# Turning float64 weights into float32: the low word rounded on ScalarE, added to the bits on GpSimd

## The chip, the core and the metric

One core of a Trainium2 chip runs the whole program. The metric is device time of one execution, in microseconds (us); the time of a kernel is the median of its runs. The engines are TensorE (PE in the profile; PEld are its weight loads), VectorE (DVE), ScalarE (ACT), GpSimd (POOL) and the queue engine SyncE (SP), which issues most transfers.

## What is computed

Three layers follow each other. A retention layer (4 batches, 8 heads, 768 positions, head size 64) keeps a decaying state and gives 3072 tokens of 512 features. A first expert layer and a second, gated one follow:

```python
def _moe_ref(x, w_in, w_out):            # 512 -> 2048 -> 512
    h = x @ w_in
    g = h * (1.0 / (1.0 + np.exp(-1.702 * h)))
    return (g @ w_out).astype(np.float32)

def _moe2_ref(x, w_gate, w_val, w_out):  # 512 -> 1536 -> 512
    gate = 1.0 / (1.0 + np.exp(-(x @ w_gate)))
    val = x @ w_val
    return (gate * val @ w_out).astype(np.float32)
```

The weights arrive as float64. The kernel gets them as 64-bit words and makes float32 values of them on the chip.

## The kernel before, in words

**Stages.** The 24 steps of 128 positions of the retention layer are cut into pieces ("items": scores, state update, output). Four steps run first, as a lead-in (9 to 26.7 us). Then 96 units follow, each one tile of 128 hidden features of the first expert layer for one block of 512 tokens: `proj` (L270) multiplies the input by the unit's weights in 12 matmuls, `gated` (L277) applies the sigmoid, and `emit_out` (L359) multiplies by the output weights, two units later (`DEPTH = 2`). Units 0 to 7 (block 0, features 0 to 7; `WHOLE`) use whole float32 output weights in slower matmuls (L375). Other operands are split into a rounded part and a rest: `split_w` (L262) casts on ACT (`wh`, L265) and subtracts on POOL or DVE (`wl`, L266). Retention items for the next block lie between the units' steps: in units 0 to 5 (block 1), and again from unit 24 on. The second expert layer fills the span from about 641 us.

**Conversion.** `stage` (L202) loads a tile of 128 x 512 words of 64 bits into one of 4 buffers. `convert` (L210) returns its steps. `scale` (ACT, L228) multiplies the upper 32 bits, read as float32, by 2^-112, which sets the exponent right. `upper` (DVE) shifts the bits left by 3 (L233) and puts the sign bit back (L236). `lower` (DVE) masks the exponent of the result (L242) and multiplies the lower 32 bits by 2^-52 and by that power of two (L246). `total` (L256) adds the two in float32. There are 68 tiles: 32 of the first layer (18 of them by the end of unit 7, two per unit in units 0 to 7 and then one per unit in units 8 to 21), whose `total` runs on POOL, and 36 of the second layer (5 in 8 units, units 22 to 79), whose `total` runs on DVE and is written to memory (`w2d`). `cva` has 3 buffers, `cvb` 2.

**Order.** The program is scheduled by hand: each engine runs its instructions in the order of the code, and a tile's readers and writers wait for each other. The loop over units (L735) puts the steps of `conv` and `conv2` between the unit's other steps:

```python
            conv[0]()          # L758: ACT, first tile
            conv2[0]()         # ACT, second tile
            conv[1]()          # DVE
            if i < FH:         # FH = 8
                conv[2]()      # DVE
                conv[3]()      # POOL
```

After these come the unit's `proj`, the split of the next unit's weights, the sigmoid and the items, and `conv2`'s remaining steps close the unit. The score matmuls (L144) share three PSUM banks `h` with `proj`, and so wait for the gate product (DVE, L284) that empties one.

Of the kernel before, what the change touches and what calls it, by code (L numbers as in the profile page):

```python
# [8 lines left out]
F32 = mybir.dt.float32  # L9
F32R = mybir.dt.float32r  # L10
U32 = mybir.dt.uint32
U64 = mybir.dt.uint64
AF = mybir.ActivationFunctionType
ALU = mybir.AluOpType

P = 128
# [8 lines left out]
def retention_moe_moe2(  # L25
# [12 lines left out]
    nc = tc.nc  # L38
# [12 lines left out]
    def pool(stack, name, bufs, side, **kw):  # L51
        return stack.enter_context(tc.tile_pool(name=name, bufs=bufs, side=side, reuse_waits="tile", **kw))
# [9 lines left out]
    cv_p = pool(right, "cv", 2, "right")  # L62
# [35 lines left out]
    def load_next(s, *parts):  # L98
        for i in parts:
            if s < NSTEP and i not in in_t.get(s, {}):  # L100
                load_in(s, i, in_p, "in")
# [23 lines left out]
    def emit_decays(c):  # L125

        for a in range(KC):
            nc.scalar.mul(dq_sb[c - 1][:, a, :], dq_sb[max(c - 2, 0)][:, a, :], dg_sb[:, a:a + 1])
# [73 lines left out]
    def stage(n=1):  # L202

        for _ in range(min(n, len(to_stage))):
            ph, f, k = to_stage.popleft()
            t = cv_p.tile([P, 512], U64, name="w64", tag="w64", bufs=4)
            nc.sync.dma_start(out=t, in_=(w1 if ph == "1" else w2)[f, k])
            staged.append((ph, f, k, t))

    def convert(n, lo_engine):  # L210

        work = []
        for _ in range(min(n, len(staged))):
            ph, f, k, t = staged.popleft()  # L220
            words = t.bitcast(U32).rearrange("p (n two) -> p n two", two=2)
            a = cv_p.tile([P, 512], F32, name="cva", tag="cva", bufs=3)
            b = cv_p.tile([P, 512], F32, name="cvb", tag="cvb")
            work.append((ph, f, k, words[:, :, 0], words[:, :, 1], a, b))

        def scale():
            for ph, f, k, lo, hi, a, b in work:
                nc.scalar.mul(a, hi.bitcast(F32), 2.0 ** -112)  # L228

        def upper():  # L230
            for ph, f, k, lo, hi, a, b in work:
                ai = a.bitcast(U32)
                nc.vector.tensor_scalar(out=ai, in0=ai, scalar1=3, scalar2=None, op0=ALU.logical_shift_left)  # L233
            for ph, f, k, lo, hi, a, b in work:
                ai = a.bitcast(U32)
                nc.vector.scalar_tensor_tensor(  # L236
                    out=ai, in0=hi, scalar=0x80000000, in1=ai, op0=ALU.bitwise_and, op1=ALU.bitwise_or
                )

        def lower():  # L240
            for ph, f, k, lo, hi, a, b in work:
                nc.vector.tensor_scalar(  # L242
                    out=b.bitcast(U32), in0=a.bitcast(U32), scalar1=0xFF800000, scalar2=None, op0=ALU.bitwise_and
                )
            for ph, f, k, lo, hi, a, b in work:
                nc.vector.scalar_tensor_tensor(  # L246
                    out=b, in0=lo, scalar=2.0 ** -52, in1=b, op0=ALU.mult, op1=ALU.mult
                )

        def total():  # L250
            for ph, f, k, lo, hi, a, b in work:
                r = a
                if ph == "1":
                    r = wraw_p.tile([P, 512], F32, name="wraw", tag="wraw")
                    raw1[f, k] = r
                lo_engine.tensor_tensor(out=r, in0=a, in1=b, op=ALU.add)  # L256
                if ph == "2":
                    nc.sync.dma_start(out=w2d[f, k], in_=r)

        return scale, upper, lower, total  # L260

    def split_w(raw, lo_engine):  # L262
        wh = wsp_p.tile([P, 512], F32R, name="wh", tag="wh")
# [39 lines left out]
    def att_items(j):  # L303

        t0, n = blocks1[j]
        items = []
        for i in range(n // C):
            s = t0 // C + i

            def first(s=s, i=i):  # L310
                if i == 0:
                    alloc_x(j)
                emit_scores(s)
                if s >= 3:
                    load_next(s + 1, KN, V)

            def second(s=s):
                emit_update(s)
                if s >= 3:
                    load_next(s + 2, Q, K)  # L320

            def third(s=s, i=i):
                if s + 1 < NSTEP:
                    emit_prep(s + 1)
                emit_y(s, *x_t[j], i * C)

            items += [first, second, third]
        return deque(items)

    FH = F1 // 2
    segments = [(b, f0, f0 + FH) for f0 in (0, FH) for b in range(2)]
    segments += [(b, 0, F1) for b in range(2, len(blocks1))]
# [13 lines left out]
    def split_for(i):  # L348

        if i < len(units):  # L350
            b, f = units[i]
            w_t[i, 0] = split_w(raw1[f, 0], nc.gpsimd if i < 3 * FH else nc.vector)
# [33 lines left out]
    def evict1(b, f):  # L386
        acc = acc_t[b]
        for c in range(4):
# [8 lines left out]
            else:  # L397
                nc.vector.tensor_copy(t, acc[c])  # L398
            nc.sync.dma_start(out=(x2d if f == F1 - 1 else halfd)[b][:, c, :], in_=t)

    NG = NT // 1024  # L410
# [9 lines left out]
    def open_early():  # L420
        p2["x"] = pool(ctx, "x2", 1, "right")
        p2["xt"] = pool(ctx, "xt", 6, "right")
        p2["w"] = [pool(ctx, "we", 1, "right")]
# [74 lines left out]
    def load_chain(n):  # L498
        if n >= len(chains):
            return  # L500
        g, r, p, m = chains[n]
        f = 2 * (r * PAIRS + p)
        t = p2["w"][n % 2].tile([P, 8, 256], F32, name="raw8", tag="raw8")
        for ff, sl in ((f + 1, slice(A21, A22 + 1, 2)), (f, slice(A11, A12 + 1))):
            nc.sync.dma_start(out=t[:, sl, :], in_=w2d[ff, m].rearrange("p (a c) -> p a c", a=2))
        wraw8[n] = t
# [172 lines left out]
    with tc.manual_schedule():  # L679
# [31 lines left out]
        parts = deque()  # L711
        for n, it in enumerate(att_items(0)):
            if n in (3, 6):
                parts.extend(convert(1, nc.gpsimd))
                stage()
                parts.popleft()()
            it()
            if n == 2:
                load_next(4, KN, V)
            if n % 3 == 1:  # L720
                for _ in range(len(parts) - 1):
                    parts.popleft()()
                emit_decays(n // 3 + 2)
            if n % 3 == 2:
                while parts:
                    parts.popleft()()
            if n in (8, 10):
                split_for((n - 8) // 2)
# [6 lines left out]
        for i, (b, f) in enumerate(units):  # L735
            if i == 0:
                items = att_items(1)
            elif (b, f) == (1, FH):
                items = att_items(2)
            elif b > 1 and f == 0:  # L740
                items = att_items(b + 1) if b + 1 < len(blocks1) else deque()
                if b == len(blocks1) - 1:
                    assert not staged and not to_stage
                    right.close()
                    open_early()
                    xs = prep_x(0)
                    load_chain(0)
            first = staged and staged[0][0] == "1"
            conv, conv2 = ([lambda: None] * 4 for _ in range(2))
            if first:  # L750
                conv = convert(1, nc.gpsimd)
                if i < FH:
                    conv2 = convert(1, nc.gpsimd)
            elif staged and (5 * i) // 8 > (5 * (i - 1)) // 8:
                conv = convert(1, nc.vector)
            xh, xl = x_t[b]
            n = blocks1[b][1]
            conv[0]()  # L758
            conv2[0]()
            conv[1]()  # L760
            if i < FH:
                conv[2]()
                conv[3]()
            hb = psum_tile("h")
            proj(hb, w_t.pop((i, 0)), xh, xl, n)
            if i > 0:
                split_for(i + 1)
            split_out(i + 1)
            if i == len(units) - 1:
                split_out(i + 2)  # L770
            g_t[i] = gated(hb, n, i < WHOLE)
            if i >= FH:
                conv[2]()
            if items and (b < 2 or f >= 1):
                items.popleft()()
            gated_lo(g_t[i], n)
            if i >= FH:
                conv[3]()
            stage(4 - len(staged))
            if items and b < 2:  # L780
                items.popleft()()
            for step in conv2[1:]:
                step()
            pend.append(i)
            while pend and i - pend[0] >= DEPTH:
                emit_out(pend.popleft())
            next(xs, None)
            if b == len(blocks1) - 1:
                if f == 9:
                    sums(0)  # L790
                elif f in (11, 13):
                    split_chain(0, f == 13)()
# [144 lines left out]
```

## Time and profile before

| | |
|---|---|
| runs | 1194.47, 1196.26, 1196.8 us; median 1196.26 |
| profiled execution | 1195.28 us, its span 1193.5 |
| TensorE busy | 1175.5 us, 98% |
| VectorE | 790.7 us, 66% |
| ScalarE | 541.4 us, 45% |
| GpSimd | 534.6 us, 45% |
| transfers | 123.48 MB, 103 GB/s over the span |

Busy shares are means over stages. A busy TensorE can be one that runs slowly: its clock has two levels, 1.2 and 2.4 GHz, and the profile gives the granted clock as a share of the higher one. The first 200 us and the rest of the span have to be read apart.

### The profile page before, as it was taken

The numbers are of one execution on the slowest core, as the hardware profiler recorded it, in microseconds if no ns is written. First come the engines' busy times: TensorE is split into PE (matmuls) and PEld (weight loads), VectorE is DVE, ScalarE is ACT, GpSimd is POOL, SyncE is SP. The second block draws the span as 40 slices with busy tenths as digits, with TensorE's granted clock in tenths as the row PEclk, the third lists the DMA queues.
The fourth block names the chain that finished last, engine by engine and source line by source line (L and its number), as shares of the span: only waits on it lengthen the run. The fifth ranks groups of instructions, "written<-read, shape, count | busy, mean of one in ns | idle before, by whom it ended". The sixth has DMA issues, their size and how long they took to land.

```text
span 1193.5 us, 16042 instructions
## 1 busy us (share of the span) xinstructions
PE 1175.5 (98%) x5916; PEld 950.4 (80%) x5916; DVE 790.7 (66%) x1050; ACT 541.4 (45%) x948; POOL 534.6 (45%) x398
## 2 busy tenths in 40 slices
PE   7999999999999999999999999999999999999998
PEld 6656878888888888888788888888888888888887
DVE  6979999676687778766664535458535458535454
ACT  5424444444444444444554626264626164626161
POOL 5557875223232332332454625257635357635340
PEclk9989999999999999999999999999999999999999
DMA  9654245533425333412202212133212133212111
GB/s 327 208 163 141 89 159 160 189 129 125 141 88 166 124 126 115 139 65 80 71 1 76 85 36 71 36 109 117 92 36 71 36 102 120 90 42 62 46 36 71
DMA packets 62575, 123.48 MB, mean 103 GB/s; under 512 B 6816, under 2 KB 16288, under 8 KB 62496
## 3 DMA queue, kind: packets, MB, share of 16 engines
q1 hardware_dynamic: 61920, 121.54, 31.4%
q8 instruction: 46, 0.75, 0.3%
q10 hardware_dynamic: 576, 0.92, 0.2%
q14 instruction: 33, 0.27, 0.1%
HBM read 98.31 MB, written 24.12 MB: 103 GB/s over the span
## 4 chain that ended last, share of the span: by engine, by line
PE 91%; DVE 5%; issue 1%; POOL 1%; DMA 1%; ACT 1%; SPq 0%; DVEq 0%; ACTq 0%; POOLq 0%
PE pa L534 16%; PE pd L534 8%; PE acc L379 7%; PE h L275 7%; PE h L274 7%; PE h L273 7%; PE acc L381 6%; PE acc L380 6%; PE po L658 4%; PE po L657 4%; PE pb L534 4%; PE po L656 4%; PE h L144 2%; PE h L185 1%; DVE cva L236 1%; PE pd L657 1%
## 5 line engine op out<-in xcount | busy, mean ns | idle before, releaser
L266 POOL TENSOR_TENSOR wl<-wraw,wh 128x512 fp32r<-128x512 f32 x112 | 166.1, 1488 | 292.7 <-ACT wh L265 292.2
L273 PE MATMUL h<-xh,wh 128*128 128x512 f32 x384 | 153.7, 400 | 0.8 <-ACT xh L189 0.7
L275 PE MATMUL h<-xh,wl 128*128 128x512 f32 x384 | 151.2, 394 | 1.8 <-POOL wl L266 1.7
L274 PE MATMUL h<-xl,wh 128*128 128x512 f32 x384 | 150.2, 391 | 0.2 <-DVE xl L190 0.2
L379 PE MATMUL acc<-gh,wh 128*128 128x512 f32 x352 | 141.8, 403 | 1.4 <-DVE half L398 1.4
L381 PE MATMUL acc<-gl,wh 128*128 128x512 f32 x352 | 137.4, 390 | 0.0
L380 PE MATMUL acc<-gh,wl 128*128 128x512 f32 x352 | 137.3, 390 | 0.0
L265 ACT CAST wh<-wraw 128x512 fp32r<-128x512 f32 x184 | 109.2, 617 | 34.9 <-PE acc L381 33.7
L526 POOL TENSOR_TENSOR ol<-raw,oh 128x768 fp32r<-128x768 f32 x36 | 66.9, 1859 | 121.2 <-ACT oh L523 121.2
L284 DVE TENSOR_TENSOR sg<-h,sg 128x512 f32<-128x512 f32 x88 | 60.5, 688 | 87.6 <-ACT sg L283 87.5
L283 ACT ACTIVATE sg<-h 128x512 f32<-128x512 f32 x88 | 52.6, 597 | 143.3 <-PE h L275 143.2
L534 PE MATMUL pa<-xoh,oh 128*128 128x512 f32 x288 | 112.5, 391 | 0.0
L534 PE MATMUL pa<-xoh,ol 128*128 128x512 f32 x288 | 112.2, 389 | 0.0
L534 PE MATMUL pa<-xol,oh 128*128 128x512 f32 x288 | 112.1, 389 | 0.0
L289 ACT CAST gh<-sg 128x512 fp32r<-128x512 f32 x88 | 54.7, 621 | 98.3 <-DVE sg L284 98.3
L646 POOL TENSOR_TENSOR wol<-wor,woh 128x512 fp32r<-128x512 f32 x36 | 57.1, 1585 | 83.0 <-ACT woh L645 83.0
L275 PEld LDWEIGHTS h<-xh,wl 128*128 128x128 f32 x384 | 72.5, 189 | 20.4 <-POOL wl L266 4.9
L273 PEld LDWEIGHTS h<-xh,wh 128*128 128x128 f32 x384 | 72.5, 189 | 17.9 <-issue 1.0
L274 PEld LDWEIGHTS h<-xl,wh 128*128 128x128 f32 x384 | 72.4, 189 | 17.4 <-issue 1.9
L236 DVE SCALAR_TENSOR_TENSOR cva<-w,cva 128x512 uint32<-128x512 uint32 x68 | 82.7, 1216 | 2.3
L656 PE MATMUL po<-woh,g2h 128*128 128x512 f32 x216 | 84.0, 389 | 0.0
L657 PE MATMUL po<-wol,g2h 128*128 128x512 f32 x216 | 84.0, 389 | 0.0
(132 smaller groups left out, 2597.2 us busy)
## 6 DMA issues: line engine op xcount, KB each, us to landing
w<-in_w_dram SPq DMA_DIRECT2D x68, 512.0 KB, 3.7
in_t<-in_qkv_dram SPq DMA_DIRECT2D x93, 256.0 KB, 3.5
raw<-w2d SPq DMA_DIRECT2D x72, 256.0 KB, 3.2
w2d<-cva SPq DMA_DIRECT2D x36, 256.0 KB, 2.2
wor<-w2d SPq DMA_DIRECT2D x36, 256.0 KB, 2.7
out_dram<-ost SPq DMA_DIRECT2D x23, 256.0 KB, 2.0
xt<-x2d SPq DMA_DIRECT2D x18, 256.0 KB, 4.2
x2d<-ost SPq DMA_DIRECT2D x14, 256.0 KB, 2.9
```

The lines of the kernel that those rows point to most:

```text
L236: nc.vector.scalar_tensor_tensor(out=ai, in0=hi, scalar=0x80000000, in1=ai, op0=ALU.bitwise_and, op1=ALU.bitwise_or)
L265: nc.scalar.copy(wh, raw)
L266: lo_engine.tensor_tensor(out=wl, in0=raw, in1=wh, op=ALU.subtract)
L273: nc.tensor.matmul(bank[:, :n], wh[:, k, :], xh[:, k, :n], start=(k == 0), stop=False)
L274: nc.tensor.matmul(bank[:, :n], wh[:, k, :], xl[:, k, :n], start=False, stop=False)
L275: nc.tensor.matmul(bank[:, :n], wl[:, k, :], xh[:, k, :n], start=False, stop=(k == KC - 1))
L379: nc.tensor.matmul(a, wh[:, wc], gh[:, :n], start=st, stop=False)
L380: nc.tensor.matmul(a, wl[:, wc], gh[:, :n], start=False, stop=False)
L381: nc.tensor.matmul(a, wh[:, wc], gl[:, :n], start=False, stop=sp)
L534: nc.tensor.matmul(bank, w[:, kk], x[:, k, :], start=start and k == 0 and w is wh and x is xh, stop=stop and k == 1 and w is wl, skip_grou ...
L656: nc.tensor.matmul(bank, gh, wh, start=f == 0, stop=False)
L657: nc.tensor.matmul(bank, gh, wl, start=False, stop=False)
```

## The change

The lower word becomes a whole number of 0 to 8 on ACT (times 2^-29, written as a 32-bit integer), and GpSimd adds it to the float32 bits as integers; a carry out of the fraction runs into the exponent, as it should. DVE's mask and product are left out, and the second layer's `total` moves from DVE to GpSimd. `scale` now issues two ACT instructions per tile; `conv` has three steps, and `total` of units 0 to 7 stands where it stood.

```diff
-    def convert(n, lo_engine):
+    def convert(n):
@@
-            b = cv_p.tile([P, 512], F32, name="cvb", tag="cvb")
+            b = cv_p.tile([P, 512], U32, name="cvb", tag="cvb")
@@ scale
                 nc.scalar.mul(a, hi.bitcast(F32), 2.0 ** -112)
+            for ph, f, k, lo, hi, a, b in work:
+                nc.scalar.mul(b, lo, 2.0 ** -29)
@@
-        def lower():
-            for ph, f, k, lo, hi, a, b in work:
-                nc.vector.tensor_scalar(
-                    out=b.bitcast(U32), in0=a.bitcast(U32), scalar1=0xFF800000, scalar2=None, op0=ALU.bitwise_and
-                )
-            for ph, f, k, lo, hi, a, b in work:
-                nc.vector.scalar_tensor_tensor(
-                    out=b, in0=lo, scalar=2.0 ** -52, in1=b, op0=ALU.mult, op1=ALU.mult
-                )
@@ total
-                lo_engine.tensor_tensor(out=r, in0=a, in1=b, op=ALU.add)
+                nc.gpsimd.tensor_tensor(out=r.bitcast(U32), in0=a.bitcast(U32), in1=b, op=ALU.add)
@@ the loop over units
-            elif staged and (5 * i) // 8 > (5 * (i - 1)) // 8:
-                conv = convert(1, nc.vector)
+            elif staged and (5 * i) // 8 > (5 * (i - 1)) // 8:
+                conv = convert(1)
@@
             if i < FH:
                 conv[2]()
-                conv[3]()
@@
             g_t[i] = gated(hb, n, i < WHOLE)
-            if i >= FH:
-                conv[2]()
@@
             if i >= FH:
-                conv[3]()
+                conv[2]()
```

How the order moves. DVE, from the gate product of unit 1 to the end of that unit's second tile (`w_` and a number is a staged tile of words; names with a number differ between the two programs). Before:

```order
L284 TENSOR_TENSOR gw<-h,gw 128x512
L190 TENSOR_TENSOR xl<-h,xh 128x4x128
L148 TENSOR_TENSOR A<-h,dm_sb 128x512 x2
L233 TENSOR_SCALAR cva<-cva 128x512
L236 SCALAR_TENSOR_TENSOR cva<-w_325,cva 128x512
L242 TENSOR_SCALAR cvb<-cva 128x512
L246 SCALAR_TENSOR_TENSOR cvb<-w_325,cvb 128x512
```

The same place in the changed program (lines there are lower by some 3 to 22):

```order
L271 TENSOR_TENSOR gw<-h,gw 128x512
L190 TENSOR_TENSOR xl<-h,xh 128x4x128
L148 TENSOR_TENSOR A<-h,dm_sb 128x512 x2
L230 TENSOR_SCALAR cva<-cva 128x512
L233 SCALAR_TENSOR_TENSOR cva<-w_324,cva 128x512
```

Two of the tile's four DVE instructions are gone; the next gate product stands that much nearer.

ACT in unit 1, from the first tile's product to the sigmoid, with what each waits for. Before:

```order
L228 ACTIVATE cva<-w_267 128x512 [waits DMAHW5_49,DVE_49]
L228 ACTIVATE cva<-w_325 128x512 [waits DMAHW6_49,Pool_49]
L265 CAST wh<-wraw 128x512
L283 ACTIVATE gw<-h 128x512 [waits PE_49]
L189 CAST xh<-h 128x4x128 [waits PE_49]
```

And in the changed program:

```order
L223 ACTIVATE cva<-w_267 128x512 [waits DMAHW5_49,DVE_49]
L225 ACTIVATE cvb<-w_267 128x512 [waits Pool_49]
L223 ACTIVATE cva<-w_324 128x512 [waits DMAHW6_49,DVE_49]
L225 ACTIVATE cvb<-w_324 128x512 [waits Pool_49]
L252 CAST wh<-wraw 128x512
L270 ACTIVATE gw<-h 128x512 [waits PE_49]
L189 CAST xh<-h 128x4x128 [waits PE_49]
```

Each tile has one more ACT instruction, and it waits for POOL, for the `total` that last read its `cvb` buffer; the cast and the sigmoid are queued behind it.

## Rows read from the trace of the kernel before

**Rows 1.** the page: busy time of each engine, then the span in 40 slices

```profile
PE 1175.5 (98%) x5916; PEld 950.4 (80%) x5916; DVE 790.7 (66%) x1050; ACT 541.4 (45%) x948; POOL 534.6 (45%) x398
PE   7999999999999999999999999999999999999998
PEclk9989999999999999999999999999999999999999
```

**Rows 2.** table of stretches, one core; columns: stretch, length, PE, PEld, DVE, ACT, POOL busy (instructions), granted clock, DMA

```profile
9.00:26.70 17.70, 13.69 (x184) 11.23 (x184) 13.92 (x20) 13.04 (x35) 12.70 (x10) 1.00 1.03 389
26.70:94.00 67.30, 62.75 (x343) 41.66 (x344) 59.31 (x82) 23.89 (x43) 36.74 (x30) 0.92 0.53 179
36.80:45.10 8.30, 6.18 (x31) 4.63 (x30) 7.51 (x13) 2.35 (x4) 4.10 (x4) 0.79 0.56 190
62.60:72.60 10.00, 7.84 (x27) 4.36 (x25) 8.49 (x13) 2.33 (x4) 5.77 (x6) 0.66 0.47 158
102.00:146.50 44.50, 44.50 (x190) 35.44 (x189) 42.98 (x48) 22.16 (x40) 36.13 (x23) 1.00 0.35 116
146.50:182.60 36.10, 34.27 (x146) 26.68 (x145) 34.97 (x39) 18.01 (x34) 28.36 (x19) 1.00 0.46 145
182.60:260.00 77.40, 77.40 (x491) 63.25 (x491) 61.73 (x90) 34.40 (x63) 25.85 (x19) 1.00 0.50 162
1000.00:1100.00 100.00, 100.00 (x443) 82.46 (x442) 55.38 (x69) 48.02 (x79) 50.64 (x41) 1.00 0.23 71
```

**Rows 3.** list of waits, TensorE: what waited for what, us in total, times, longest

```profile
PE h L144 <- DVE gw L284: 4.1, 2, 2.2
PE acc L185 <- DVE A L148: 1.7, 4, 0.7
PE h L275 <- POOL wl L266: 1.7, 4, 1.2
PE acc L178 <- POOL qs L120: 1.7, 2, 1.0
PE acc L379 <- DVE half L398: 1.4, 1, 1.4
```

**Rows 4.** one line at a time: min/median/max duration in ns, first and last start, shapes

```profile
L233 DVE TENSOR_SCALAR cva<-cva x68: 416/421/1550, 13.9 to 551.3; 128x512 uint32<-128x512 uint32 x68
L236 DVE SCALAR_TENSOR_TENSOR cva<-w,cva x68: 691/1640/1822, 14.3 to 551.8; 128x512 uint32<-128x512 uint32 x68
L242 DVE TENSOR_SCALAR cvb<-cva x68: 408/426/1291, 15.0 to 555.4; 128x512 uint32<-128x512 uint32 x68
L246 DVE SCALAR_TENSOR_TENSOR cvb<-w,cvb x68: 691/693/1637, 15.5 to 555.8; 128x512 f32<-128x512 uint32 x68
L284 DVE TENSOR_TENSOR sg<-h,sg x88: 675/691/694, 100.0 to 642.8; 128x512 f32<-128x512 f32 x88
L296 DVE TENSOR_TENSOR gl<-sg,gh x88: 679/684/1522, 102.1 to 644.2; 128x512 fp32r<-128x512 f32 x88
L256 DVE TENSOR_TENSOR cva<-cva,cvb x36: 681/683/686, 189.4 to 557.0; 128x512 f32<-128x512 f32 x36
L256 POOL TENSOR_TENSOR wraw<-cva,cvb x32: 1266/1392/1678, 18.0 to 180.0; 128x512 f32<-128x512 f32 x32
L266 POOL TENSOR_TENSOR wl<-wraw,wh x112: 1268/1455/1849, 24.4 to 641.0; 128x512 fp32r<-128x512 f32 x112
L228 ACT ACTIVATE cva<-w x68: 656/671/694, 13.0 to 550.6; 128x512 f32<-128x512 f32 x68
```

**Rows 5.** timeline, VectorE and GpSimd, around 170 to 175 us

```profile
170.20 1.66 DVE L236 SCALAR_TENSOR_TENSOR cva<-w,cva 128x512 uint32<-128x512 uint32 x1
174.10 1.67 POOL L256 TENSOR_TENSOR wraw<-cva,cvb 128x512 f32<-128x512 f32 x1 [1.09 <-DVE cvb L246]
```

**Rows 6.** timeline, ScalarE, at 57.8 us

```profile
57.85 0.69 ACT L228 ACTIVATE cva<-w 128x512 f32<-128x512 f32 x1 [1.03 <-POOL wraw L256]
```

**Rows 7.** timeline, VectorE, attention lead-in

```profile
21.50 1.64 DVE L246 SCALAR_TENSOR_TENSOR cvb<-w,cvb 128x512 f32<-128x512 uint32 x1
```

More of the change, by code (lines that the diff above doesn't have):

```diff
@@ L255, in total @@
                     raw1[f, k] = r
-                lo_engine.tensor_tensor(out=r, in0=a, in1=b, op=ALU.add)
+                nc.gpsimd.tensor_tensor(out=r.bitcast(U32), in0=a.bitcast(U32), in1=b, op=ALU.add)
                 if ph == "2":
                     nc.sync.dma_start(out=w2d[f, k], in_=r)
-        return scale, upper, lower, total
+        return scale, upper, total
     def split_w(raw, lo_engine):
@@ L713, in retention_moe_moe2 @@
             if n in (3, 6):
-                parts.extend(convert(1, nc.gpsimd))
+                parts.extend(convert(1))
                 stage()
@@ L748, in retention_moe_moe2 @@
             first = staged and staged[0][0] == "1"
-            conv, conv2 = ([lambda: None] * 4 for _ in range(2))
+            conv, conv2 = ([lambda: None] * 3 for _ in range(2))
             if first:
-                conv = convert(1, nc.gpsimd)
+                conv = convert(1)
                 if i < FH:
-                    conv2 = convert(1, nc.gpsimd)
+                    conv2 = convert(1)
             elif staged and (5 * i) // 8 > (5 * (i - 1)) // 8:
-                conv = convert(1, nc.vector)
+                conv = convert(1)
             xh, xl = x_t[b]
```

## The prediction

> **What bounds the kernel now.** First the page: TensorE is busy 98% of the span, and what it lacks lies almost wholly in the first slices and the last one; the granted clock too is below full only early on [rows 1]. Only the first 183 us and the tail can therefore give anything. Second, the table of stretches, for TensorE's busy time and clock: from 182.6 us on there is no idle time and no lower clock [rows 2]. At full pace 100 us hold 443 of the 512-column matmuls, 0.226 us each [rows 2]. Third, the list of TensorE's waits: all of it is early, and most is for VectorE, directly (4.1 us for the gate product that empties a bank, 1.7 for the score product) or through GpSimd [rows 3].
>
> Fourth, why VectorE is late. Read each line's fastest and median duration [rows 4]. The sign merge (L236) takes 0.69 us at best and 1.64 in the median; the shift (L233), the mask (L242) and the low-word product (L246) have the same two faces, 0.41 to 0.69 against 1.29 to 1.64. The gate product (L284), which reads a PSUM bank, never leaves 0.68 to 0.69. On GpSimd the same add takes from 1.27 to 1.68. The timeline shows the pattern: a sign merge started at 170.20 lasts 1.66 us beside GpSimd's subtractions, and GpSimd then stands 1.09 us, until the low-word product is done, before its add can start [rows 5]. So VectorE's SBUF-only instructions and GpSimd's take turns, and the conversion chain bounces between them. In 146.5 to 182.6 VectorE is busy 34.97 of 36.10 us and GpSimd 28.36 [rows 2]: together more than the stretch, partly counting each other's blocking.
>
> **The change, part by part.**
>
> *Removed from VectorE:* 68 masks at 0.43 and 68 low-word products at 0.69 us, 76 us at medians [rows 4], more with the blocking, and 36 adds of the second layer at 0.683, 24.6 us [rows 4]. What of it is on the path is priced by the losses of TensorE below.
>
> *Added to ScalarE:* 68 products, strided words in, 512 elements out. Nearest row: the existing product, same stride, 0.671 us [rows 4]; 45.6 us in all. The forecast takes that. In 26.7 to 94 us it is 16 x 0.67 = 10.7 us on an engine busy 23.89 of 67.30 [rows 2], so the time is covered; the new wait is not. The product writes a buffer of which there are two, so it waits for GpSimd's add of two tiles earlier, with the weight cast and the sigmoid queued behind it. Nearest row: the existing product already waits 1.03 us for such an add [rows 6]. Bounds: nothing (the add is done in time), or 1 us in each of units 0 to 7, 8 us. I charge 0.9 us once, in unit 1, where the retention scores need the bank that the sigmoid frees and no output matmuls yet lie between; 0.5 in unit 4, which has the same order of banks.
>
> *The integer add on GpSimd,* no row shows it. Nearest row: the float32 add of the same shape, 1.27 us unblocked, 1.39 median [rows 4]; the other end is twice that, 2.6 us. I take the float add's price: same operands, same bytes. GPSIMD Engine Reference of the Trainium skill, section Engine selection, states that such an add comes out exact and wrapping where all three operands are 32-bit integers; it gives no price, and no run here shows it.
>
> *The 36 adds moved from VectorE to GpSimd* cost 0.683 us where they were and 1.27 to 1.68 where they go [rows 4], 46 to 60 us more work for GpSimd between 189 and 557 us. In 182.6 to 260 GpSimd is busy 25.85 of 77.40 us and TensorE never waits [rows 2]; output products lie two units behind, and nothing here is on the path. I price it at 0; if the cover failed, the excess of about 0.7 us each would be 25 us. The Trainium skill speaks against this step: the same section of GPSIMD Engine Reference says to put two-input elementwise work on VectorE, GpSimd being about twice as slow. The rows agree on the ratio; by that rule the sum would lose those 25 us, by the stretch nothing.
>
> *What TensorE gets back.*
> 1. Lead-in, 9 to 26.7 us. Waits for the score product 1.7 and for GpSimd's scaled queries 1.7 us [rows 3], 3.4 at most. The third of these steps stands behind a low-word product that took 1.64 us from 21.50 on [rows 7]. Loads and ScalarE's state copies come next. I take 1.0.
> 2. Unit 1, 36.8 to 45.1. Idle 8.30 - 6.18 = 2.12; clock 0.79, so 8.30 x 0.21 = 1.74 more: 3.86 [rows 2]. Less the 0.9 for the new wait: 2.9.
> 3. Unit 4, 62.6 to 72.6. Idle 2.16, clock 0.66: 10 x 0.34 = 3.4; together 5.56 [rows 2]. The clock fell after TensorE had stood waiting for the gate product (longest 2.2 us [rows 3]); without the stand it should hold. Less 0.5: 5.0.
> 4. Around 96 us, 1.2 us for a weight rest from GpSimd [rows 3]. I take 1.0.
> 5. 146.5 to 182.6: 146 matmuls at 0.226 are 33.0 us, the stretch takes 36.1, so 3.1 are lost, the 1.4 us wait for an eviction among them [rows 2, 3]. Until 146.5 TensorE lived on a lead it had built up. I take 2.6.
>
> Check that GpSimd and VectorE together now fit under TensorE. 26.7 to 94: GpSimd 36.7, and 16 shifts and sign merges at 0.42 + 0.69 = 17.8, together 54.5; TensorE without its losses needs 67.3 - 3.86 - 5.56 = 57.9 [rows 2, 4]. 102 to 182.6: 41 GpSimd instructions at 1.27 are 52.1, the remaining VectorE ones (13 shifts and merges, 15 rests L296 at 0.68) 24.6, sum 76.7; the 13 removed pairs were 14.3, so 91.0 ran in 80.6 us, a factor 0.886 for overlap at the turns; 76.7 x 0.886 = 68.0 against TensorE's 77.5. Both fit. In the first stretch the add may cost 1.27 + 0.2, roughly, before GpSimd shows, and 2.1 before all is given back.
>
> Sum: 1.0 + 2.9 + 5.0 + 1.0 + 2.6 = 12.5 us. The profiled execution took 1195.28 us (span 1193.5), so 1182.8; the median of the runs lies 0.98 above that execution, which gives **1183.8 us**. From 183 us on TensorE works without a gap, so all that is won early arrives at the end.
>
> **The rivals.**
>
> *ScalarE's new wait takes VectorE's place.* Per unit a ring forms: GpSimd's second add, ScalarE's product, cast and sigmoid, gate product, retention work, shift and merge, add. For it: the two buffers, and a wait of 1.03 us of the kind already there [rows 6]. Against it: about 6 us of links for a unit of 8. At 0.8 us in each of 8 units it eats 6.4: 1190. Its span is 1188 to 1194.
>
> *The integer add is slower than the float add.* This is the side of slower. From 2.1 us on GpSimd is the bound in units 0 to 7, worse than VectorE was. At 2.6 us: first stretch 54.5 + 16 x 1.27 = 74.8 against 67.3 now, +7.5; second 68.0 + 14 x 1.33 x 0.886 = 84.5 against 80.6, +3.9; two adds in the lead-in, about +1: 1196.3 + 12.4 = 1208.7. For it: nothing in the trace runs integers on GpSimd. Against it: its float instructions with two inputs all take 1.27 at best, whatever they compute [rows 4].
>
> *The moved adds block VectorE after 183 us.* A victim loses up to 1.64 - 0.69 = 0.95 us [rows 4]; 36 adds, a third of them exposed, 11 us, which cancels the gain: 1195. Against it: 15.7 us of VectorE's 77.4 are free there [rows 2], and it loses 113 us of work. SBUF — State Buffer, section Who interferes with whom, of the Trainium skill has the rule: a VectorE instruction with two SBUF inputs, or in a two-port mode, and a GpSimd instruction that reads SBUF exclude each other for a whole instruction. The fastest and slowest durations here agree with it.
>
> **How the numbers follow.** Forecast 0.66, ScalarE's wait 0.15, moved adds (or a gain that another early limit, such as the loads, swallows) 0.06, slower add 0.13. A measurement of this kernel can tell about 0.2%, 2.4 us. Low end: all losses whole, 3.4 + 3.86 + 5.56 + 1.2 + 3.1 = 17.1, hence 1179.1. High end 1193.5 takes in ScalarE's wait; the slower add and the cancelled gain, 0.19, are left out. Faster 0.81 (forecast and ScalarE's wait), same 0.06, slower 0.13. The forecast's own range is 1179 to 1188.
>
> **What would show it.** Right: the gate product's waits on TensorE's list gone, the clock full from 36 to 73 us, VectorE's busy time lower by over 100 us, the integer add at 1.3 to 1.5 us, the stretch from 182.6 us unchanged in length and begun some 12 us earlier. Wrong: the integer add above 2 us; a wait of ScalarE's second product for GpSimd over 1 us in most early units with TensorE waiting for the sigmoid; or any wait of TensorE after 183 us.

## The result, and the profile after

The changed kernel takes 1180.69 us (median of 4 runs, 1180.4 to 1182.65) against 1195.89 for the kernel before (4 runs, 1194.47 to 1196.8). The ratio is 0.9877, its 95% interval 0.986 to 0.9895: 15.2 us less. The profiled execution took 1180.4 us, its span 1178.6.

The page of the changed kernel: busy time of each engine, TensorE's slices, its granted clock.

```profile
PE 1168.6 (99%) x5916; PEld 948.5 (80%) x5916; DVE 641.7 (54%) x878; ACT 580.3 (49%) x1016; POOL 558.9 (47%) x434
PE   8999999999999999999999999999999999999998
PEclk9999999999999999999999999999999999999999
```

VectorE is busy 149 us less than in [rows 1]'s kernel, though the instructions that left it make only 99 us at their fastest durations; the rest is time in which it had stood blocked. The clock's digit is 9, the highest, in every slice.

The table of stretches of the changed kernel (stretch, length, then PE, PEld, DVE, ACT, POOL busy, granted clock, DMA). The first stretch is units 0 to 7, the second units 17 to 22, the third the one shown before.

```profile
25.00:84.00 59.00, 58.00 (x345) 39.25 (x345) 39.26 (x55) 33.42 (x61) 39.28 (x32) 1.00 0.65 224
134.70:167.40 32.70, 32.70 (x146) 27.06 (x146) 18.58 (x25) 20.41 (x38) 23.91 (x17) 1.00 0.44 145
182.60:260.00 77.40, 77.40 (x493) 62.98 (x491) 44.80 (x68) 38.19 (x69) 32.44 (x26) 1.00 0.49 161
```

Units 0 to 7 take 59 us, where they took 67.3 at a clock of 0.92 [rows 2]. The 146 matmuls that took 36.1 us with TensorE idle for 1.83 take 32.7 without a gap. From 182.6 to 260 us TensorE is busy throughout in both kernels, though GpSimd does 6.6 us more there (the work in this stretch is not quite the same, as all of it now comes 15 us earlier).

TensorE's list of waits, changed kernel, three of its early entries:

```profile
PE acc L178 <- POOL qs L120: 1.0, 2, 0.5
PE acc L185 <- DVE A L148: 0.9, 2, 0.7
PE h L144 <- DVE gw L271: 0.7, 1, 0.7
```

The wait for the gate product is 0.7 us, once, where it was 4.1 [rows 3]; those for the weight rest and for the eviction are gone.

One line at a time, changed kernel (minimum, median, maximum in ns): shift, sign merge, ScalarE's new product, the integer add of the second and of the first layer, GpSimd's weight rests.

```profile
L230 DVE TENSOR_SCALAR cva<-cva x68: 413/420/1486, 13.9 to 536.1; 128x512 uint32<-128x512 uint32 x68
L233 DVE SCALAR_TENSOR_TENSOR cva<-w,cva x68: 691/693/1668, 14.3 to 536.5; 128x512 uint32<-128x512 uint32 x68
L225 ACT ACTIVATE cvb<-w x68: 651/664/700, 13.5 to 535.9; 128x512 uint32<-128x512 uint32 x68
L243 POOL TENSOR_TENSOR cva<-cva,cvb x36: 1272/1285/1722, 170.5 to 538.9; 128x512 uint32<-128x512 uint32 x36
L243 POOL TENSOR_TENSOR wraw<-cva,cvb x32: 1265/1298/1808, 17.3 to 160.7; 128x512 uint32<-128x512 uint32 x32
L253 POOL TENSOR_TENSOR wl<-wraw,wh x112: 1267/1296/1825, 23.2 to 625.8; 128x512 fp32r<-128x512 f32 x112
```

Two prices that no row of before had are now there. The integer add costs what the float add costs: 1.27 us at best, 1.29 to 1.30 in the median. ScalarE's product of strided integers costs 0.66 us. And the sign merge's median over all 68 tiles, 1.64 us before [rows 4], is 0.69: it mostly no longer meets a GpSimd instruction. In units 0 to 7 it still does, and half of the merges there are stretched:

```profile
L233 DVE SCALAR_TENSOR_TENSOR cva<-w,cva x17: 691/1555/1668, 27.0 to 83.8; 128x512 uint32<-128x512 uint32 x17
```

So the turns are not gone from these units; there are fewer of them.

Where the 15 us came from is read best from the start of the first matmul of unit 0 and of unit 23, in TensorE's timeline. Before:

```profile
26.75 0.50 PE L273 MATMUL h<-xh,wh 128*128 128x512 f32 x1 [0.68 <-ACT xh L189]
182.43 0.39 PE L273 MATMUL h<-xh,wh 128*128 128x512 f32 x1
```

After:

```profile
25.07 0.50 PE L260 MATMUL h<-xh,wh 128*128 128x512 f32 x1 [0.68 <-ACT xh L189]
167.40 0.39 PE L260 MATMUL h<-xh,wh 128*128 128x512 f32 x1
```

Lead-in: 1.7 us less. Units 0 to 22: 155.7 us before, 142.3 now, 13.4 less. From unit 23 to the end of the span: 1011.1 before, 1011.2 now. The sum is the difference of the spans, 14.9 us. All experiments below use this measure as well as the time, because the lead-in's end moves by itself: in four profiles of kernels with one and the same lead-in, unit 0 begins at 25.07, 25.68, 26.11 and 26.12 us.

### The profile page after: what moved, and what is told of

It is laid out like the page before. It is cut to its first block, busy times and chain, and to the rows that moved or that the text cites. A ratio compares the mean times of both kernels' runs of the same rounds, so it can differ in the third digit from the quotient of the medians.

```text
span 1178.6 us, 16028 instructions
## 1 busy us (share of the span) xinstructions
PE 1168.6 (99%) x5916; PEld 948.5 (80%) x5916; DVE 641.7 (54%) x878; ACT 580.3 (49%) x1016; POOL 558.9 (47%) x434
## 4 chain that ended last, share of the span: by engine, by line
PE 96%; DMA 2%; DVE 1%; ACT 0%; POOL 0%; issue 0%; ACTq 0%; SPq 0%; DVEq 0%; POOLq 0%
PE pa L512 17%; PE pd L512 8%; PE acc L365 7%; PE h L262 7%; PE h L261 7%; PE h L260 7%; PE acc L367 7%; PE acc L366 7%; PE po L635 4%; PE po L634 4%; PE pb L512 4%; PE po L636 4%; PE acc L361 2%; PE h L144 2%; PE h L185 2%; PE pd L635 1%
## 5 line engine op out<-in xcount | busy, mean ns | idle before, releaser
L253 POOL TENSOR_TENSOR wl<-wraw,wh 128x512 fp32r<-128x512 f32 x112 | 151.0, 1354 | 282.1 <-ACT wh L252 259.4
L270 ACT ACTIVATE sg<-h 128x512 f32<-128x512 f32 x88 | 52.6, 598 | 145.2 <-PE h L262 144.9
L283 DVE TENSOR_TENSOR gl<-sg,gh 128x512 fp32r<-128x512 f32 x88 | 69.9, 795 | 41.2 <-ACT gh L276 41.2
```

The source lines that it names most:

```text
L253: lo_engine.tensor_tensor(out=wl, in0=raw, in1=wh, op=ALU.subtract)
L283: nc.vector.tensor_tensor(out=gl[:, :n], in0=sg[:, :n], in1=gh[:, :n], op=ALU.subtract)
```

## The experiments

The theory: in units 0 to 22, and only there, VectorE's instructions that read SBUF alone (the on-chip memory that holds the tiles, as against the PSUM banks) and GpSimd's take turns, that is, one stands while the other runs; mask and product took turns too, and made the units longer than TensorE needs. Rivals: the relief after 183 us, VectorE's time as such, the add's wait for the product, or the longer hold of the staged tile.

**The changed kernel again**, as a base for the next run.

> The changed kernel once more, for comparison with the next one on the same chip. All theories: 1180.7 us within 2, ratio 0.987 to 0.988.

Measured 1180.41 us (1180.37 to 1180.99), ratio 0.988 [0.9863, 0.9896]; units 0 to 22 take 142.4 us.

**Only the move of the 36 adds**, on the kernel before.

```diff
-                conv = convert(1, nc.vector)
+                conv = convert(1, nc.gpsimd)
```

> The kernel before, with only the 36 float adds of the second layer moved from VectorE to GpSimd. My theory (nothing after 183 us is on the path): 1195.9 us within 2.4, no wait of TensorE after 183 us. Rival, the move gives part of the gain: 1191 or less. Rival, the moved adds block VectorE and show: 1199 or more.

Measured 1195.52 us, ratio 1.0005 [0.9995, 1.0014]. TensorE still waits 4.1 us for the gate product. The moved add and the stretch from 182.6 us on:

```profile
L256 POOL TENSOR_TENSOR cva<-cva,cvb x36: 1291/1671/1685, 189.0 to 557.6; 128x512 f32<-128x512 f32 x36
182.60:260.00 77.40, 77.40 (x491) 63.22 (x491) 59.55 (x83) 34.29 (x63) 36.57 (x26) 1.00 0.48 159
```

An add of 0.68 us on VectorE became one of 1.67 on GpSimd, and TensorE is busy 77.40 of 77.40 us all the same. One part of the expectation did not hold: in this profile TensorE does wait once after 183 us, 0.5 us for a weight rest from VectorE at 473 us, and the span from unit 23 on is 1012.1 us instead of 1011.1. Shortly before, VectorE and ScalarE had stood 4.1 and 5.2 us for a store, and the changed kernel, which has the move too, shows no such wait. In the time the move is worth nothing, and a cost is not resolved: the interval leaves -0.6 to 1.7 us.

**The new conversion in the first layer alone.** The second layer keeps mask, product and VectorE's add.

```diff
-            b = cv_p.tile([P, 512], F32, name="cvb", tag="cvb")
+            b = cv_p.tile([P, 512], U32 if ph == "1" else F32, name="cvb", tag="cvb")
@@ scale
+                if ph == "1":
+                    nc.scalar.mul(b, lo, 2.0 ** -29)
@@ lower
+            if work and work[0][0] == "1":
+                return
@@ total
+                if ph == "1":
+                    nc.gpsimd.tensor_tensor(out=r.bitcast(U32), in0=a.bitcast(U32), in1=b, op=ALU.add)
+                else:
+                    lo_engine.tensor_tensor(out=r, in0=a, in1=b, op=ALU.add)
```

> The new conversion for the first layer's 32 tiles alone; the second layer's 36 tiles are converted as before (mask and product on VectorE, float add on VectorE). My theory: the whole gain, 1180.7 us within 2. Rival, relief of VectorE after 183 us matters too: 1184 or more.

Measured 1180.59 us, ratio 0.9881 [0.9867, 0.9896]; units 0 to 22 take 142.3 us. The 32 tiles of the first layer carry the whole gain; the other 36 could have been left as they were.

**Mask and product put back, for nobody.** The new conversion stays; the pair writes into words of the staged tile that nobody reads afterwards.

```diff
+        def lower():
+            for ph, f, k, lo, hi, a, b in work:
+                nc.vector.tensor_scalar(
+                    out=hi, in0=a.bitcast(U32), scalar1=0xFF800000, scalar2=None, op0=ALU.bitwise_and
+                )
+            for ph, f, k, lo, hi, a, b in work:
+                nc.vector.scalar_tensor_tensor(
+                    out=hi.bitcast(F32), in0=lo, scalar=2.0 ** -52, in1=hi.bitcast(F32), op0=ALU.mult, op1=ALU.mult
+                )
```

> The changed kernel with the mask and the product put back on VectorE where they stood, writing into words of the staged tile that nobody reads afterwards; the total doesn't use them. Wanted: is it VectorE's turns with GpSimd that cost, or only that the add waited for the product? If the turns cost (my theory), most of the gain is lost: 1188 to 1196. If only the add's wait for the product cost, 1181 to 1183.

Measured 1198.85 us, ratio 1.0027 [1.0018, 1.0037]: the whole gain is gone, and a little more, outside the range given. Units 0 to 22 are back at 155.5 us; the little more is the lead-in (unit 0 begins at 29.80 us), which now holds the pair and ScalarE's product. In this profile the lead-in also ran at a granted clock of 0.69 from 9 to 20 us, where the kernel before had 1.00; what each adds is not separated. Unit 0 and unit 23, the pair's durations, and the waits:

```profile
29.80 0.50 PE L275 MATMUL h<-xh,wh 128*128 128x512 f32 x1 [0.68 <-ACT xh L189]
185.31 0.39 PE L275 MATMUL h<-xh,wh 128*128 128x512 f32 x1
```

```profile
L244 DVE TENSOR_SCALAR w<-cva x68: 409/427/1393, 17.1 to 558.2; 128x512 uint32<-128x512 uint32 x68
L248 DVE SCALAR_TENSOR_TENSOR w<-w x68: 692/694/1674, 18.3 to 558.7; 128x512 f32<-128x512 uint32 x68
```

```profile
PE h L144 <- DVE gw L286: 5.0, 2, 2.6
PE h L277 <- POOL wl L268: 3.0, 4, 1.0
PE acc L185 <- DVE A L148: 2.8, 4, 1.8
PE acc L381 <- ACT wh L267: 2.4, 1, 2.4
```

GpSimd's add of the first layer no longer waits for the product, and still nothing is won. So that wait alone, which the timeline of before showed [rows 5], was not the cause: where it is gone, the pair's own turns cost as much. In the kernel before, the wait stood in the place of the product's turns. There the product was never stretched in units 0 to 22, and GpSimd stood until it was done (the product's durations from 27 to 183 us, and GpSimd's wait for it, in us and times):

```profile
L246 DVE SCALAR_TENSOR_TENSOR cvb<-w,cvb x30: 691/693/704, 30.5 to 179.2; 128x512 f32<-128x512 uint32 x30
  POOL wraw L256: 44.8, 27
```

Either way the two engines work one after the other. No run has the wait without the turns, so what each cost in the kernel before stays open.

**Reductions in place of the pair.** Two maxima over the converted tile, into a spare column: one SBUF input, one output column.

```diff
+        def lower():
+            for ph, f, k, lo, hi, a, b in work:
+                s = cv_p.tile([P, 2], F32, name="scr", tag="scr", bufs=1)
+                for j in range(2):
+                    nc.vector.tensor_reduce(out=s[:, j:j + 1], in_=a, axis=mybir.AxisListType.X, op=ALU.max)
```

> As the run with the spare pair, but instead of mask and product two reductions (maximum over the converted tile's 512 values) into a spare column: about as much VectorE time (I expect 0.55 to 0.65 us each), one input, one output column. If taking turns with GpSimd is what costs, these don't wait for GpSimd (fastest and slowest duration alike) and most of the gain stays: 1181 to 1187. If VectorE's time as such costs, it is as slow as the spare pair, 1188 to 1196.

Measured 1182.92 us, ratio 0.9895 [0.988, 0.991]. Units 0 to 22 take 142.6 us. The reductions' durations, and the two ends:

```profile
L246 DVE TENSOR_REDUCE scr<-cva x136: 669/676/686, 15.6 to 543.6; 128x1 f32<-128x512 f32 x136
```

```profile
25.65 0.49 PE L271 MATMUL h<-xh,wh 128*128 128x512 f32 x1 [0.69 <-ACT xh L189]
168.28 0.39 PE L271 MATMUL h<-xh,wh 128*128 128x512 f32 x1
```

Each tile has 1.35 us more of VectorE, more than the pair's 1.12, and 136 instructions lie between 0.669 and 0.686: not one was blocked. The gain stays. VectorE's time as such was not the bound. Of the 2.2 us by which this kernel's time lies above the changed kernel's, 1.6 lie behind unit 23 (1012.8 us to the end of the span, against 1011.2), where TensorE waits 0.7 us for an eviction and 0.5 us for a weight cast; the next run does not have them (1011.0).

**The same reductions over the staged tile's upper words**, which hold that tile as long as the pair does.

```diff
+                for j, x in enumerate((hi, hi)):
+                    nc.vector.tensor_reduce(
+                        out=s[:, j:j + 1], in_=x.bitcast(F32), axis=mybir.AxisListType.X, op=ALU.max
+                    )
```

> As the run with reductions, but they read the staged tile's upper words, so that the staged tile is held as long as with the spare pair. If the spare pair cost because it takes turns with GpSimd: 1181 to 1185. If it cost because it holds the staged tile, and so the loads, longer: 1190 or more.

Measured 1181.37 us, ratio 0.9878 [0.9863, 0.9893]; units 0 to 22: 142.5 us. The hold of the staged tile costs nothing.

**The mask alone, and the product alone,** as spare instructions (the product then takes the converted tile as its second input).

```diff
+                nc.vector.tensor_scalar(
+                    out=hi, in0=a.bitcast(U32), scalar1=0xFF800000, scalar2=None, op0=ALU.bitwise_and
+                )
@@ or, in the other kernel
+                nc.vector.scalar_tensor_tensor(
+                    out=hi.bitcast(F32), in0=lo, scalar=2.0 ** -52, in1=a, op0=ALU.mult, op1=ALU.mult
+                )
```

> The changed kernel with only the spare mask (one SBUF input, 0.42 us alone) put back on VectorE. The mask too showed two faces in the kernel before (0.41 and 1.29 us), so it should cost: stretch from unit 0 to unit 23 between 143 and 150 us (142.3 without, 155.5 with the pair), time 1181 to 1189. If only instructions with two SBUF inputs take turns: 1180.7 to 1182.

> The changed kernel with only the spare product (two SBUF inputs, 0.69 us alone) put back. If what counts is each instruction's turn, about the other part of the pair's loss: stretch from unit 0 to unit 23 between 144 and 152 us, time 1183 to 1191, and the two parts together make the pair's 13 us. If the loss sets in only when GpSimd's and VectorE's turns together fill a unit, each part alone costs much less than half of it.

Mask alone: 1181.1 us, ratio 0.9876 [0.9861, 0.989], units 0 to 22 142.5 us. That misses the 143 to 150 that I gave. The time would also fit the other reading, that only instructions with two SBUF inputs take turns, but the mask's durations don't: from 0.41 us up to 1.46, and 12 of the 15 masks in units 8 to 22 took over 0.49.

```profile
L244 DVE TENSOR_SCALAR w<-cva x68: 412/428/1461, 15.5 to 541.6; 128x512 uint32<-128x512 uint32 x68
```

Product alone: 1184.32 us, ratio 0.9902 [0.9885, 0.9918], 145.2 us. The stretch from 100 to 160 us of four kernels, one fence each; after, then with the mask, with the product, with the pair:

```profile
100.00:160.00 60.00, 60.00 (x267) 49.69 (x266) 34.99 (x46) 38.46 (x69) 47.04 (x35) 1.00 0.42 137
```

```profile
100.00:160.00 60.00, 60.00 (x267) 49.68 (x266) 54.92 (x56) 37.76 (x68) 46.42 (x33) 1.00 0.41 137
```

```profile
100.00:160.00 60.00, 59.23 (x261) 48.59 (x260) 57.95 (x57) 36.97 (x67) 46.76 (x32) 1.00 0.43 141
```

```profile
100.00:160.00 60.00, 56.74 (x232) 42.74 (x230) 59.31 (x64) 34.52 (x63) 42.36 (x29) 1.00 0.33 105
```

The fifth column is VectorE: 34.99, 54.92, 57.95, 59.31 of 60 us, most of the growth blocked time. TensorE (third column) notices only when VectorE has next to nothing left: 60.00, 60.00, 59.23, 56.74. In units 0 to 22 the mask costs 0.1 us, the product 2.9, both together 13.2. The parts don't add up; that the loss sets in where the turns fill the unit is worked out in the section on what to carry. The table splits units 0 to 22 where unit 8 starts.

| kernel | unit 0 starts | unit 23 starts | units 0 to 22 | units 0 to 7 | units 8 to 22 | time |
|---|---|---|---|---|---|---|
| before | 26.75 | 182.43 | 155.7 | 67.3 | 88.4 | 1195.89 |
| after | 25.07 | 167.40 | 142.3 | 58.9 | 83.5 | 1180.69 |
| after, spare mask | 26.34 | 168.79 | 142.5 | 59.0 | 83.5 | 1181.10 |
| after, spare product | 26.99 | 172.20 | 145.2 | 60.2 | 85.0 | 1184.32 |
| after, both | 29.80 | 185.31 | 155.5 | 65.4 | 90.1 | 1198.85 |
| after, two reductions | 25.65 | 168.28 | 142.6 | 59.2 | 83.5 | 1182.92 |
| after, one low-word buffer | 26.53 | 179.98 | 153.5 | 70.0 | 83.5 | 1192.00 |

**ScalarE's product without its wait,** on the kernel before, with a result that nobody reads.

```diff
+            for ph, f, k, lo, hi, a, b in work:
+                s = cv_p.tile([P, 512], mybir.dt.bfloat16, name="scr", tag="scr", bufs=1)
+                nc.scalar.mul(s, lo, 2.0 ** -29)
```

> The kernel before with ScalarE's low-word product added for all 68 tiles, its result unused (16-bit output into a spare tile): the price of ScalarE's work without its wait. My theory: 1195.9 us within 2.4. If ScalarE's time is near the path, 1198 to 1203.

Measured 1195.27 us, ratio 0.9995 [0.9983, 1.0008]. ScalarE is busy 579.2 us instead of 541.4, and that is covered.

**One buffer for the low word instead of two**, so that ScalarE's product waits for the add of the tile just before.

```diff
-            b = cv_p.tile([P, 512], U32, name="cvb", tag="cvb")
+            b = cv_p.tile([P, 512], U32, name="cvb", tag="cvb", bufs=1)
```

> The changed kernel with one buffer for the low word instead of two: ScalarE's low-word product then waits for GpSimd's add of the tile just before, in every unit. If the ring over ScalarE is near the path (two buffers just suffice), the sigmoid comes some 2 us late in units 0 to 7 and 3 to 12 us are lost: 1184 to 1193. If ScalarE has ample slack, under 2 us: 1181 to 1183.

Measured 1192.0 us, ratio 0.9968 [0.9958, 0.9978]: 11 of the 15 us are lost, all in units 0 to 7. ScalarE's wait for the add, with one buffer, in the list of waits up to 200 us; TensorE's; and two stretches:

```profile
ACT cvb L225 <- POOL wraw L243: 52.3, 28, 5.3
```

```profile
PE h L144 <- DVE gw L271: 5.4, 2, 3.0
PE h L260 <- DVE gw L271: 1.7, 1, 1.7
```

```profile
34.00:46.00 12.00, 9.02 (x59) 7.32 (x58) 8.05 (x14) 4.07 (x8) 5.89 (x5) 0.89 0.49 178
58.00:72.00 14.00, 11.61 (x55) 7.44 (x54) 8.76 (x14) 5.95 (x12) 7.62 (x7) 0.83 0.54 187
```

With two buffers, up to 200 us, the same wait of ScalarE is this:

```profile
ACT cvb L225 <- POOL wraw L243: 15.1, 7, 3.4
```

So the ring over ScalarE is real, and two buffers nearly suffice. The clock falls below full again, around units 1 and 4, as it did before the change [rows 2], after TensorE had stood 3.0 and 2.4 us for the gate product. This time VectorE itself stood 3.4 us before each of these two products, until the sigmoid was done, so it was ScalarE that made TensorE stand.

**The low-word product of the second tile behind the sigmoid**, units 0 to 7. The product becomes a step of its own, `conv[1]`; the steps behind it move up by one.

```diff
             conv[0]()
+            conv[1]()
             conv2[0]()
@@
             g_t[i] = gated(hb, n, i < WHOLE)
+            conv2[1]()
```

> The changed kernel with ScalarE's low-word product of each unit's second tile moved behind that unit's sigmoid (units 0 to 7). If the product's wait for GpSimd's add is what makes TensorE stand 0.7 us for the gate product in unit 1 and run 0.45 us late in unit 4, both go and the time falls by 0.8 to 1.3 us, to about 1179.7. If that stand comes from VectorE instead (gate product queued behind shift and merge that GpSimd blocks), nothing changes: 1180.7. If a late product makes GpSimd's second add late instead, the weight rest for a later unit is late and the time rises by 1 to 3 us.

Measured 1180.57 us (1179.78 to 1180.9), ratio 0.988 [0.9866, 0.9895], against 1180.41 for the changed kernel on the same chip: no difference in the time. Unit 1's wait for the gate product is gone from TensorE's list, and unit 1 takes 6.36 us from its first matmul to unit 2's, against 7.17; units 0 to 22 take 141.6 us against 142.4. Unit 4 takes 8.97 us with and without the edit, so only the first of the two losses that the expectation put down to this wait comes from it. These 0.8 us are less than the scatter of the lead-in's end, and no run shows them in the time.

## Why the prediction was right

The forecast was 12.5 us less, 1183.8; measured are 15.2 less. The mechanism is the one given, and most of its steps have their run; one term, unit 4's, met its number for another reason, and one reading of the rows does not hold.

- *Nothing after 183 us is on the path; the 36 moved adds cost 0.* Right: the move alone gives 1.0005, with up to 1.7 us left open by its interval, and the span from unit 23 on is 1011.1 and 1011.2 us before and after. The rule that the Trainium skill gives in GPSIMD Engine Reference, section Engine selection (two-input work belongs on VectorE, GpSimd being about twice as slow), describes the duration, 1.67 against 0.68 us, and not the time of this kernel: GpSimd's excess is covered.
- *The integer add costs what the float add costs.* Right: 1.29 to 1.30 us in the median. The rival of the slower side needed 2.1 and falls. (Its sum of 1208.7 charged 1.27 us more per add in the first stretch and 1.33 in the second; with 1.33 in both it is 1209.7.)
- *The turns of VectorE and GpSimd fit under TensorE once the pair is gone.* Right: reductions of more VectorE time keep the gain, the spare pair loses it. SBUF — State Buffer, section Who interferes with whom, of the Trainium skill says that reductions never contend and that a VectorE instruction with two SBUF inputs does; the durations agree (0.669 to 0.686 against 0.692 to 1.674 us).
- *VectorE's products make GpSimd wait*, as the prediction read from the 1.09 us before the add [rows 5]: true of the trace, and not the cause by itself. With that wait gone and the pair's turns left, units 0 to 22 take 155.5 us. The prediction also gave the low-word product the same two faces as the others; its slow face, 1.64 us, belongs to the lead-in alone, and in units 0 to 22 none of 30 products took more than 0.704.
- *ScalarE's new wait costs 0.9 us in unit 1 and 0.5 in unit 4.* Right for unit 1: TensorE waited 0.7 us there, and no longer does with the product behind the sigmoid. For unit 4 the number came out by luck. Its scores took 0.45 us more than undisturbed ones (1.54 against 1.09 us in the timeline), but they do so with the product moved as well. In both kernels ScalarE stood idle before that unit's sigmoid, until TensorE's own matmuls were done (changed kernel, then the one with the late product):

```profile
56.85 0.60 ACT L270 ACTIVATE gw<-h 128x512 f32<-128x512 f32 x1 [1.05 <-PE h L262]
57.12 0.60 ACT L272 ACTIVATE gw<-h 128x512 f32<-128x512 f32 x1 [3.28 <-PE h L264]
```

  So the new wait did not cost anything there. With one buffer the rival had its full force, 11 us.
- *The sizes of TensorE's losses.* From unit 1 to unit 3, 18.31 us before and 15.18 now: 3.1 back, 2.9 forecast. Unit 4: 14.26 and 8.97, 5.3 back, 5.0 forecast. The first matmuls of units 1, 3, 4 and 5, before and after:

```profile
31.89 0.50 PE L273 MATMUL h<-xh,wh 128*128 128x512 f32 x1
50.20 0.80 PE L273 MATMUL h<-xh,wh 128*128 128x512 f32 x1
58.30 0.79 PE L273 MATMUL h<-xh,wh 128*128 128x512 f32 x1
72.56 0.80 PE L273 MATMUL h<-xh,wh 128*128 128x512 f32 x1
```

```profile
30.21 0.50 PE L260 MATMUL h<-xh,wh 128*128 128x512 f32 x1
45.39 0.80 PE L260 MATMUL h<-xh,wh 128*128 128x512 f32 x1
53.48 0.79 PE L260 MATMUL h<-xh,wh 128*128 128x512 f32 x1
62.45 0.79 PE L260 MATMUL h<-xh,wh 128*128 128x512 f32 x1
```

  These hold idle time and lower clock together; the clock is full in 25 to 84 us. The clock's share is not separated, and it may be worth less than the prediction's sum gives it: in one set of runs of the kernel before, those at a mean clock of 0.999 took 1194.6 us on average (3 runs) and those at 0.996 took 1195.4 (4 runs), in another set 1195.0 (3) and 1196.7 (10). The difference of 0.003 is 3.6 us of the span and goes with 0.8 to 1.7 us of time.

By these terms 15.0 us came back, 2.5 more than forecast; 2.0 of them lie in three terms that I had cut below their bounds, the rest in units 1 and 4. Units 17 to 22 gave 3.4 and not 2.6, more than the bound of 3.1, which counted matmul records at 0.226 us each, some of them outside these units. The wait around 96 us gave 1.5 and not 1.0 (units 8 and 9 took 13.83 us before and 12.33 now); that the restart after the wait goes with it is not shown. The lead-in gave 1.7 in this profile and not 1.0. In the two profiles with the lead-in of before, unit 0 begins at 26.64 and 26.75 us, in the four with the new one at 25.75 on average, so about 1.0 us is the better figure.

## What to carry to other kernels

Where an instruction's median is far above its fastest duration and its neighbour on another engine has the same two faces, add up the two engines' undisturbed durations in one unit of work, shorten the sum by what the turns overlap, and compare it with what the bound engine needs. The plain sum says too much. In units 11 to 22 of the changed kernel TensorE needs 5.44 us from one unit to the next. Three GpSimd instructions at 1.27 us and VectorE's shift, merge and rest (0.42, 0.69, 0.68) make 5.60, and yet the changed kernel loses nothing there. With the overlap of the kernel before, which the prediction put at a factor of 0.886 from one stretch, it is 4.96; with the mask 5.34, with the product 5.57, with both 5.95. For the 14 tiles of units 8 to 21 that gives an estimate of no loss, no loss, 1.9 and 7.2 us; units 8 to 22 lost 0, 0, 1.5 and 6.6. Below the bound extra work was free, and above it nearly all of the excess showed. Moving a pass to an engine with slack pays by the turns that it frees, not by its duration. And a buffer that carries a result between two engines needs the count that lets both run ahead: here two left less than 1 us of loss and one lost 11 us.

## What was not expected

- The spare mask, 0.42 us alone, raised VectorE's busy time between 100 and 160 us from 34.99 to 54.92 us, as it waited in GpSimd's shadow, and cost TensorE 0.1 us in 23 units. A VectorE that is 92% busy was not the bound here.
- The loss of the pair (13.2 us) is more than four times the sum of its parts (0.1 and 2.9).
